# The long convolution of an H3 block recast from a 64x32 to a 128x16 split, with half of its shift filter moved to the tensor engine

## The chip, the cores and the metric

One core of one Trainium2 chip runs the whole program. The metric is device microseconds of one execution; lower is better. The old kernel took 296.26 us (median of 2 runs, 295.95 to 296.57). Engines are named as in the profile: PE is TensorE (matrix products), PEld its weight loads, DVE is VectorE, ACT is ScalarE, POOL is GpSimd, SP is the engine that issues most DMAs. "L498" is line 498 of the kernel that was run.

## The reference, cut to what matters

Four layers with residuals: mixer A, MLP B, A, B. The tensors are 2048 tokens by 512 channels, bf16. The convolution part of A depends on k, v and fixed weights, not on x, so both kernels compute it once and use it for both A layers.

```python
def _A_ref(q, k, v, shift_k, ssm_k, ssm_D):
    k_shift = sum over t in 0..3 of k_pad[:, t:t+S, :] * shift_k[:, 3-t]   # 4-tap causal filter
    kv = k_shift * v
    y = irfft(rfft(pad(kv)) * rfft(pad(ssm_k)))[:S]      # causal convolution of length 2048, per channel
    y = y + kv * ssm_D
    return q * y
def _B_ref(x, w1, b1, w2, b2):
    return gelu(layernorm(x) @ w1 + b1) @ w2 + b2        # 512 -> 1376 -> 512
x = x + A(layernorm(x)); x = x + B(layernorm(x)); x = x + A(...); x = x + B(...)
```

## The kernel before

The kernel records operations with declared durations, and a list scheduler written in the kernel file fixes the order of each engine before the program is built. So an edit can also re-order work. `A(p0, n, off, dims)` is a region of one big SBUF array, `P.op(engines, fn, duration, ...)` records one operation.

The convolution is a Fourier transform in two steps, as matrix products. A token index is 32c + a (c in 0..63, a in 0..31). Data sit as two groups of 64 partitions, so k and v are loaded in halves of 64 partitions:

```python
for g in range(2):
    dma(A(64 * g, 64, R_K + 1536, [1, 8192]), dr(A_k, 16 * g * 512, [32 * 512, 64], [1, 8192]), 1 << 20)
for g in range(2):
    dma(A(64 * g, 64, R_V, [1, 8192]), dr(A_v, 16 * g * 512, [32 * 512, 64], [1, 8192]), 1 << 20)
for j in range(8):
    tload(t_s2, 64 * 384, j * 3072, R_S2 + j * 3072, 3072)      # stage-two table, 6.3 MB
```

The shift filter runs on VectorE: seven tensor_tensor of 2048 columns and two of 1024 for each of four chunks:

```python
def shift_chunk(w):
    ...
    for j in range(3):
        tap(3 - j, tm[j])                       # multiply by one tap, 128x2048
    tt(tm[1], tm[0], tm[1], ALU.add, 1140.0)
    tap(0, tm[0])
    tt(tm[2], tm[1], tm[2], ALU.add, 1140.0)
    tt(tm[1], tm[2], tm[0], ALU.add, 1140.0)
    for h in range(2):
        tt(..., R_TMP ..., R_V ..., ALU.mult, 610.0)            # times v
    stage1(R_KP, R_GX + 8192 * (w // 2), 64, ..., EV_X)         # EV_X = (ACT,): evictions on ScalarE
```

Real and imaginary parts lie in columns of the same partition. Stage two takes three matmuls for each frequency, and the complex product takes two multiplies and an add and a subtract on VectorE:

```python
for i, t, gg in ins:                            # stage2, for each frequency
    e.matmul(Q(tl, 0, 128, i * 2 * n, [1, 2 * n]), t[0], gg[0], start=True, stop=False)
    e.matmul(Q(tl, 0, 128, i * 2 * n, [1, n]), t[1], gg[1], start=False, stop=False)
    r = e.matmul(Q(tl, 0, 128, i * 2 * n + n, [1, n]), t[2], gg[2], start=False, stop=True)
...
tt(po, x3, H, ALU.mult, 600.0)                  # products, for each 8 frequencies
tt(x3, x3, H_swapped_by_access_pattern, ALU.mult, 600.0)
for ri, p in ((0, po), (1, xo)):
    tt(R_Y ..., p[:32], p[32:], ALU.add if ri else ALU.subtract, 330.0)
```

After the inverse transform come the layer norms and the four MLP blocks per layer; the change leaves their arithmetic alone.

Of the kernel before, what the change touches and what calls it, by code (L numbers as in the profile page):

```python
# [7 lines left out]
ALU = mybir.AluOpType  # L8
# [371 lines left out]
def _tables():  # L380

    c = np.arange(64)[:, None]
    k1 = np.arange(64)[None, :]
    th = TWO_PI * c * (k1 + 0.5) / 128
    F = np.stack([np.cos(th), -np.sin(th)], -1).reshape(64, 128)
    F = np.concatenate([F, F], 0)
    a = np.arange(32)
    k2 = np.arange(32)
    f = np.arange(64)[:, None] + 0.5 + 128 * k2[None, :]
    th = TWO_PI * a[:, None, None] * f[None] / 4096  # L390
    tr = np.stack([np.cos(th), np.sin(th), -np.sin(th)], 2)
    S2 = np.zeros((32, 4, 64, 3, 32, 4))
    for d in range(4):
        S2[:, d, :, :, :, d] = tr
    S2 = S2.reshape(128, 64 * 3 * 128)
    ph = TWO_PI * k2[:, None] * a[None, :] / 32
    U = np.zeros((32, 4, 2, 32, 2, 4))
    for d in range(4):
        U[:, d, 0, :, 0, d] = np.cos(ph)
        U[:, d, 0, :, 1, d] = np.sin(ph)  # L400
        U[:, d, 1, :, 0, d] = -np.sin(ph)
        U[:, d, 1, :, 1, d] = np.cos(ph)
    U = U.reshape(128, 512)
    t = 32 * np.arange(64)[None, :] + a[:, None]
    ps = TWO_PI * t[None] * (np.arange(64)[:, None, None] + 0.5) / 4096
    T2 = np.stack([np.cos(ps), -np.sin(ps)], 2) / 2048
    T2 = T2.reshape(64, 4096)
    T2 = np.concatenate([T2, T2], 0)
    return F, S2, U, T2


AR = 105984


def bass_interleave_layers__ssm_conv_h3__mixer_channel_mlp__prompt_kernel(
# [3 lines left out]
    NS = 192  # L419
# [23 lines left out]
    def place(n):  # L443
        o = pos[0]
        pos[0] += n
        return o

    R_ID, R_F, R_D, R_B1, R_SJ3 = place(128), place(128), place(16), place(16), place(512)
    R_S2 = place(64 * 384)
    R_1, R_2, R_3, R_4, R_5, R_6 = (place(n) for n in (16384, 16384, 17920, 16384, 8192, 5120))  # L450
    assert pos[0] <= AR, pos[0]
    R_HRAW, R_HP, R_H = R_1, R_1 + 8192, R_1
    R_W1, R_W2 = R_1, R_1 + 5504
    R_GH, R_Z = R_2, R_2
    R_K, R_V, R_Y, R_U = R_3, R_3 + 19 * 512, R_3, R_3 + 16384
    R_GX, R_SR, R_X, R_T2 = R_4, R_4 + 12288, R_4, R_4 + 8192
    R_SJ = [R_4 + 8192 + 512 * w for w in range(3)] + [R_SJ3]
    R_KP, R_YT = R_5, R_5
    R_TMP, R_RING = R_6, R_6
    R_XT = R_S2  # L460
    R_HT = R_S2 + 4096
    R_N = R_S2 + 4096 + 2 * 5632
    M_B1, M_ST, M_MV, M_RS, M_HF = 0, 16, 16 + 96, 16 + 96 + 32, 16 + 96 + 32 + 16

# [4 lines left out]
    def dma(dst, src, nbytes, reads=(), prio=0.0, writes=None):  # L469
        return P.op(SP, lambda e: e.dma_start(dst, src, allow_slow_non_contiguous=True), 550.0, reads=reads,  # L470
                    writes=[dst] if writes is None else writes, dma=True, nbytes=nbytes, prio=prio)
# [7 lines left out]


    row = 128 + 128 + 512 + 4096
    P.op(ACT, lambda e: e.preload_act_table(AF.Gelu_apprx_tanh), 1300.0, prio=1e6)
    z = A(0, 1, R_K, [1, 1536])
    P.op(POOL, lambda e, z=z: e.memset(z, 0.0), 1300.0, writes=[z])
    tload(t_sm, row, 0, R_ID, 256)
# [3 lines left out]
    dma(A(0, 128, R_SR, [1, 2048]), dr(A_shift_k, 0, [0, 128], [1, 2048]), 1 << 19)  # L489
    dma(A(64, 64, R_K, [1, 1536]), dr(A_k, 13 * 512, [32 * 512, 64], [1, 1536]), 3 << 16)  # L490
    dma(A(1, 63, R_K, [1, 1536]), dr(A_k, 29 * 512, [32 * 512, 63], [1, 1536]), 3 << 16)
    for g in range(2):
        dma(A(64 * g, 64, R_K + 1536, [1, 8192]), dr(A_k, 16 * g * 512, [32 * 512, 64], [1, 8192]), 1 << 20)
    for g in range(2):
        dma(A(64 * g, 64, R_V, [1, 8192]), dr(A_v, 16 * g * 512, [32 * 512, 64], [1, 8192]), 1 << 20)
    for j in range(8):
        tload(t_s2, 64 * 384, j * 3072, R_S2 + j * 3072, 3072)

    HP = 0.0
    EV_H = EV_X = (ACT,)  # L500
    IDN = A(0, 128, R_ID, [1, 128])
    dconv, dx = Pool(2, 4), Pool(2, 2)
# [4 lines left out]
    P.op(POOL, lambda e: e.tensor_tensor(d0, d0, dd, ALU.add), 600.0, reads=[d0, dd], writes=[d0])  # L507
    for a4 in range(4):
        tl = Tile(dconv)
        for al in range(4):  # L510
            ins = []
            for b in range(4):
                for g in range(2):
                    src = A(0, 128, R_HRAW + b * 2048 + 16 * g + 4 * a4 + al, [32, 64])
                    ins.append((g, al * 512 + b * 128, src))

            def f(e, ins=ins, tl=tl):
                for g, o, src in ins:
                    r = e.transpose(QB(tl, 64 * g, 64, o, [1, 128]), src, IDN)
                return r  # L520
            P.op(PE, f, 8 * 60.0, reads=[x[2] for x in ins] + [IDN], tile=tl)
        dst = A(0, 128, R_HP + 16 * a4, [4, 4], [64, 128], [1, 4])

        def f(e, dst=dst, tl=tl):
            src = QB(tl, 0, 128, 0, [512, 4], [4, 128], [1, 4])
            if e is nc.scalar:
                return e.activation(dst, src, AF.Copy)
            return e.tensor_copy(dst, src)
        P.op((ACT, DVE), f, {ACT: 2048 * .833 + 60, DVE: 2048 * .52 + 70}, writes=[dst], tile=tl)

    def stage1(src, G, gk, gh, dg0, n, engs, prio=0.0):


        for d8 in range(dg0 // 8, (dg0 + n) // 8):
            for h in range(2):
                tl = Tile(dconv)
                ins = [(64 * g, i, A(64 * g, 64, src + (64 * h + 8 * d8 + i) * 64, [1, 64]), A(64 * g, 64, R_F, [1, 128]))
                       for i in range(8) for g in range(2)]

                def f(e, ins=ins, tl=tl):  # L540
                    for p, i, w, m in ins:
                        r = e.matmul(Q(tl, p, 64, i * 128, [1, 128]), w, m, start=True, stop=True)  # L542
                    return r
                P.op(PE, f, 16 * 45.0, reads=[x for y in ins for x in y[2:]], tile=tl, prio=prio)
                dst = A(0, 128, G + gh(h, 8 * d8), [gk, 128], [1, 8])

                def f(e, dst=dst, tl=tl):
                    src = Q(tl, 0, 128, 0, [1, 128], [128, 8])
                    if e is nc.scalar:
                        return e.activation(dst, src, AF.Copy)  # L550
                    return e.tensor_copy(dst, src)
                P.op(engs, f, {ACT: 1100.0, DVE: 1024 * 1.04 + 90}, writes=[dst], tile=tl, prio=prio)

    def stage2(G, ks, n, pool, prio=0.0):

        tl = Tile(pool)
        ins = []
        for i, k1 in enumerate(ks):
            g = G + k1 * 2 * n
            t = [A(0, 128, R_S2 + k1 * 384 + j * 128, [1, 128]) for j in range(3)]  # L560
            gg = [A(0, 128, g, [1, 2 * n]), A(0, 128, g + n, [1, n]), A(0, 128, g, [1, n])]
            ins.append((i, t, gg))

        def f(e):
            for i, t, gg in ins:
                e.matmul(Q(tl, 0, 128, i * 2 * n, [1, 2 * n]), t[0], gg[0], start=True, stop=False)  # L566
                e.matmul(Q(tl, 0, 128, i * 2 * n, [1, n]), t[1], gg[1], start=False, stop=False)  # L567
                r = e.matmul(Q(tl, 0, 128, i * 2 * n + n, [1, n]), t[2], gg[2], start=False, stop=True)  # L568
            return r
        P.op(PE, f, len(ks) * (4 * n * .42 + 10), reads=[x for _, t, gg in ins for x in t + gg[:1]], tile=tl, prio=prio)  # L570
        return tl

    stage1(R_HP, R_GH, 128, lambda h, dg: 64 * (dg // 32) + 32 * h + dg % 32, 0, 64, EV_H, HP)
    for k4 in range(16):
        tl = stage2(R_GH, range(4 * k4, 4 * k4 + 4), 128, dconv, HP)
        dst = A(0, 128, R_H + k4 * 1024, [1, 1024])

        def f(e, dst=dst, tl=tl):
            src = Q(tl, 0, 128, 0, [1, 1024])
            if e is nc.scalar:  # L580
                return e.activation(dst, src, AF.Copy)  # L581
            return e.tensor_copy(dst, src)  # L582
        P.op((ACT, DVE), f, {ACT: 1024 * .833 + 60, DVE: 1024 * 1.04 + 70}, writes=[dst], tile=tl, prio=HP)


    def tt(o, a, b, op, dur, eng=DVE):
        return P.op(eng, lambda e: e.tensor_tensor(o, a, b, op), dur, reads=[a, b], writes=[o])  # L587

# [4 lines left out]

    def shift_chunk(w):

        tm = [A(0, 128, R_KP + w * 1024, [64, 16], [4096, 2], [1, 64])]
        tm += [A(0, 128, o, [128, 16], [64, 2], [1, 64]) for o in (R_TMP, R_TMP + 2048)]

        def tap(j, o):
# [260 lines left out]
```

## Time and profile before

| stretch | what it is | what is full |
|---|---|---|
| 0 to 25.4 us | loads, filter transform begins | DMA |
| 25.4 to 121.5 us | convolution | VectorE, with ScalarE behind it |
| 121.5 to 295 us | layer norms and MLP | TensorE from 151 on |

The page of the old kernel, first its busy totals, then busy tenths in 40 slices of 7.4 us, and what the DMA engines moved in each slice:

```profile
PE 240.2 (81%) x2177; PEld 138.1 (47%) x2192; DVE 189.4 (64%) x401; ACT 143.0 (48%) x176; POOL 24.1 (8%) x43
DVE  0135999999999998898890794874938611101131
ACT  1069079598968469616327045152366321464000
GB/s 203 297 213 213 224 414 284 2 18 6 2 224 296 197 97 2 1 5 69 51 20 2 71 0 28 46 0 63 8 2 71 18 53 2 71 0 2 71 71 71
```

VectorE is at 8 or 9 tenths from the fifth to the sixteenth slice. In the table of stretches, the columns are busy time and instruction count of each engine, granted TensorE clock, DMA share and GB/s (two short rows between the stages are left out):

```profile
core 0: us, PE busy (x) PEld busy (x) DVE busy (x) ACT busy (x) POOL busy (x), PEclk, DMA share, GB/s
0.00:25.40 25.40, 11.83 (x256) 10.91 (x256) 3.82 (x7) 9.54 (x9) 1.88 (x7) 1.00 0.92 233
25.40:66.00 40.60, 25.70 (x474) 21.78 (x475) 39.88 (x39) 28.13 (x31) 0.96 (x2) 0.83 0.62 194
66.00:101.10 35.10, 30.02 (x554) 27.87 (x551) 34.73 (x65) 28.49 (x31) 1.04 (x2) 0.99 0.50 134
151.00:289.00 138.00, 137.26 (x612) 57.13 (x625) 64.58 (x163) 51.57 (x77) 10.81 (x18) 1.00 0.15 31
```

In the first row the DMA engines are busy for 0.92 of the time. VectorE then works 39.88 of 40.6 us and 34.73 of 35.1 us; from 151 to 289 TensorE works 137.26 of 138. What VectorE does, from the groups by form (count, then busy us and mean ns, then idle before them and its releaser):

```profile
L587 DVE TENSOR_TENSOR ar<-ar 128x512 bf16<-128x512 bf16 x96 | 35.1, 416 | 1.4 <-ACT ar L712 1.4
L587 DVE TENSOR_TENSOR ar<-ar 128x2048 bf16<-128x2048 bf16 x28 | 32.9, 1220 | 7.3 <-DMA ar<-in_A_k_dram 7.0
L587 DVE TENSOR_TENSOR ar<-ar 128x1024 bf16<-128x1024 bf16 x40 | 25.9, 683 | 0.2
L550 ACT ACTIVATE ar<-ps 128x1024 bf16<-128x1024 f32 x32 | 30.0, 1050 | 12.7 <-PE ps L542 12.7
```

Of the 96 adds and multiplies of 512 columns, 32 belong to the complex product. The 28 of 2048 columns are the shift filter. And from the timeline of VectorE and of ScalarE (start, length, group, idle before it and what ended that), where the shift filter begins and where the convolution's last evictions are:

```profile
25.38 38.18 DVE L587 TENSOR_TENSOR ar<-ar 128x2048 bf16<-128x2048 bf16 x36 [7.04 <-DMA ar<-in_A_k_dram]
...
114.10 7.44 ACT L712 ACTIVATE ar<-ps 128x1024 bf16<-128x1024 f32 x8 [0.74 <-PE ps L704]
```

The filter begins at 25.38 us, after waiting for k. The last eviction ends at 114.10 + 7.44 = 121.54 us.

### The profile page before, as it was taken

What the parts mean: (1) busy time and instruction counts of PE and PEld (TensorE: products, weight loads), DVE (VectorE), ACT (ScalarE), POOL (GpSimd) and SP (SyncE); (2) the same over time, 40 slices, a digit from 0 to 9 for tenths busy, and PEclk for the clock granted to TensorE, in tenths of its full rate; (3) what the DMA queues carried; (4) which work ended last, traced back from release to release, by engine and by line L of the source; (5) the groups of instructions that cost most, each with busy time, mean ns of one, the idle gap of its engine ahead of it and who ended that gap; (6) DMA issues with size and microseconds to landing.
All of it is one profiled execution on the core that took longest, in us unless ns stands there. A gap on an engine that the chain in (4) does not pass through costs nothing.

```text
span 295.0 us, 5161 instructions
## 1 busy us (share of the span) xinstructions
PE 240.2 (81%) x2177; PEld 138.1 (47%) x2192; DVE 189.4 (64%) x401; ACT 143.0 (48%) x176; POOL 24.1 (8%) x43
## 2 busy tenths in 40 slices
PE   0657086799899396329999999999999999999992
PEld 0655075588799284113433434434433444434440
DVE  0135999999999998898890794874938611101131
ACT  1069079598968469616327045152366321464000
POOL 2000000100010022210210110111101100000000
PEclk9999658999999879758999999999999999999997
DMA  6999997000099520003210301303003020200322
GB/s 203 297 213 213 224 414 284 2 18 6 2 224 296 197 97 2 1 5 69 51 20 2 71 0 28 46 0 63 8 2 71 18 53 2 71 0 2 71 71 71
DMA packets 22703, 25.75 MB, mean 87 GB/s; under 512 B 17722, under 2 KB 19355, under 8 KB 22170
## 3 DMA queue, kind: packets, MB, share of 16 engines
q1 hardware_dynamic: 22682, 25.44, 33.0%
q8 instruction: 17, 0.28, 0.4%
q14 instruction: 4, 0.03, 0.0%
HBM read 19.66 MB, written 2.10 MB: 74 GB/s over the span
## 4 chain that ended last, share of the span: by engine, by line
PE 51%; DVE 24%; DMA 10%; ACT 7%; SPq 2%; issue 2%; POOL 2%
PE ps L818 24%; PE ps L800 23%; DVE ar L587 16%; DMA ar<-in_A_v_dram 10%; DVE sm L729 3%; ACT ar L581 2%; SPq L470 2%; ACT ar L658 2%; DVE ar L743 2%; PE ps L650 2%; ACT ar L550 2%; ACT ar L627 1%; POOL sm L737 1%; DVE ar L582 1%; PE ps L566 1%
## 5 line engine op out<-in xcount | busy, mean ns | idle before, releaser
L805 ACT ACTIVATE ar<-ps,sm 128x512 bf16<-128x512 f32 (+1 forms) x88 | 59.5, 686 | 82.3 <-PE ps L800 59.1
L587 DVE TENSOR_TENSOR ar<-ar 128x512 bf16<-128x512 bf16 (+2 forms) x164 | 91.5, 618 | 8.9 <-DMA ar<-in_A_k_dram 7.0
L800 PE MATMUL ps<-ar 128*128 128x512 bf16 (+1 forms) x342 | 81.7, 385 | 1.6 <-ACT ar L789 1.2
L818 PE MATMUL ps<-ar 128*128 128x512 bf16 (+1 forms) x347 | 78.1, 379 | 0.8 <-DVE ar L822 0.6
L822 DVE TENSOR_TENSOR ar<-ar,ps 128x512 bf16<-128x512 bf16 x32 | 21.2, 682 | 65.5 <-PE ps L818 65.5
L800 PEld LDWEIGHTS ps<-ar 128*128 128x128 bf16 (+1 forms) x352 | 30.8, 101 | 50.8 <-ACT ar L805 21.4
L818 PEld LDWEIGHTS ps<-ar 128*128 128x128 bf16 (+1 forms) x352 | 33.6, 98 | 43.4 <-ACT ar L805 2.9
L729 DVE BATCH_NORM_STATS2 sm<-ar 128x6 f32<-128x512 bf16 x64 | 41.4, 681 | 0.1
L550 ACT ACTIVATE ar<-ps 128x1024 bf16<-128x1024 f32 x32 | 30.0, 1050 | 12.7 <-PE ps L542 12.7
L542 PE MATMUL ps<-ar 64*64 64x128 bf16 x512 | 21.6, 241 | 17.3 <-DVE ar L587 10.9
L566 PE MATMUL ps<-ar 128*128 128x128 bf16 (+1 forms) x192 | 30.0, 239 | 2.3 <-ACT ar L550 1.5
L743 DVE TENSOR_SCALAR ar<-ar,sm 128x512 bf16<-128x512 bf16 x64 | 23.2, 406 | 11.4 <-POOL sm L737 10.3
L568 PE MATMUL ps<-ar 128*128 128x64 bf16 (+1 forms) x192 | 29.2, 202 | 0.0
L567 PE MATMUL ps<-ar 128*128 128x64 bf16 (+1 forms) x192 | 29.1, 201 | 0.0
L542 PEld LDWEIGHTS ps<-ar 64*64 64x64 bf16 x512 | 17.9, 121 | 20.9 <-issue 9.1
L650 PE MATMUL ps<-ar 128*128 128x256 bf16 x128 | 17.7, 301 | 5.5 <-DVE ar L587 5.2
L566 PEld LDWEIGHTS ps<-ar 128*128 128x128 bf16 x192 | 18.7, 98 | 4.3 <-ACT ar L550 2.1
L568 PEld LDWEIGHTS ps<-ar 128*128 128x128 bf16 x192 | 18.8, 98 | 0.7
L650 PEld LDWEIGHTS ps<-ar 128*128 128x128 bf16 x128 | 15.7, 175 | 7.0 <-DVE ar L587 5.5
L567 PEld LDWEIGHTS ps<-ar 128*128 128x128 bf16 x192 | 18.8, 98 | 0.0
L627 ACT ACTIVATE ar<-ps 128x1024 bf16<-128x1024 f32 x16 | 15.9, 1043 | 3.3 <-DVE ar L587 3.1
L658 ACT ACTIVATE ar<-ps 128x1024 bf16<-128x1024 f32 x14 | 13.7, 1042 | 7.9 <-PE ps L650 7.9
(27 smaller groups left out, 97.0 us busy)
## 6 DMA issues: line engine op xcount, KB each, us to landing
ar<-tab_s SPq DMA_DIRECT2D x8, 768.0 KB, 34.1
ar<-in_A_ssm_k_dram SPq DMA_DIRECT2D x4, 512.0 KB, 5.5
ar<-in_A_k_dram SPq DMA_DIRECT2D x2, 1024.0 KB, 16.3
ar<-in_A_v_dram SPq DMA_DIRECT2D x2, 1024.0 KB, 25.9
ar<-in_A_q_dram SPq DMA_DIRECT2D x2, 1024.0 KB, 10.5
out_dram<-ar SPq DMA_DIRECT2D x8, 256.0 KB, 3.1
ar<-in_B_w_dram SPq DMA_DIRECT2D x1, 1376.0 KB, 8.5
ar<-in_B_w_dram SPq DMA_DIRECT2D x1, 1280.0 KB, 6.1
```

Of the source, the lines that this page charges most:

```text
L542: r = e.matmul(Q(tl, p, 64, i * 128, [1, 128]), w, m, start=True, stop=True)
L550: return e.activation(dst, src, AF.Copy)
L566: e.matmul(Q(tl, 0, 128, i * 2 * n, [1, 2 * n]), t[0], gg[0], start=True, stop=False)
L567: e.matmul(Q(tl, 0, 128, i * 2 * n, [1, n]), t[1], gg[1], start=False, stop=False)
L568: r = e.matmul(Q(tl, 0, 128, i * 2 * n + n, [1, n]), t[2], gg[2], start=False, stop=True)
L587: return P.op(eng, lambda e: e.tensor_tensor(o, a, b, op), dur, reads=[a, b], writes=[o])
L650: r = e.matmul(Q(tl, 0, 128, i * 256, [1, 256]), w, m, start=ri == 0, stop=ri == 1)
L729: P.op(DVE, lambda e, st=st, x=x: e.bn_stats(st, x), 600.0, reads=[x], writes=[st])
L743: P.op(DVE, lambda e: e.tensor_scalar(o, x, m, r, ALU.subtract, ALU.mult), 260.0, reads=[x, m, r], writes=[o])
L800: r = e.matmul(Q(tl, 0, rows, 0, [1, 512]), w, m, start=dk == 0, stop=dk == 3)
L805: P.op(ACT, lambda e, dst=dst, tl=tl, rows=rows, bias=bias: e.activation(dst, Q(tl, 0, rows, 0, [1, 512]), AF.Gelu_apprx_tanh, bias=bias), ...
L818: r = e.matmul(Q(tl, 0, 128, 0, [1, 512]), ins[fc][0], ins[fc][1], start=fc == 0, stop=fc == 10)
```

## The change

The token index becomes 16b + a (b in 0..127), so that every partition holds one block of 16 consecutive tokens and all loads span 128 partitions. Real parts lie on partitions 0-63, imaginary ones on 64-127, so stage two is one full 128x128 matmul for each frequency, with a table of 4 MB in place of 6.3. The complex product becomes two multiplies, by the spectrum H and by HS, a copy of it with the halves exchanged; the add and subtract are folded into the inverse matmul. HS is made by four 1 MB copies inside SBUF. Half of the channels (two of four blocks of 128) have their shift filter done on TensorE, with k transposed by the DMA and diagonal weight matrices. Evictions (the copies of finished sums out of PSUM, TensorE's output memory) of the first stage and of the products, on ScalarE alone before, may now go to VectorE too.

```diff
-R_K + 1536, two loads of 64 partitions;  R_V, two loads of 64 partitions
+    for i, c in enumerate(PE_CH):                     # PE_CH = (0, 1)
+        dst = A(0, 128, R_KT + i * 2064 + 16, [2048, 1], [1, 2048])
+        src = dr(A_k, 128 * c, [512, 2048], [1, 128])
+        P.op(SP, lambda e, dst=dst, src=src: e.dma_start_transpose(dst, src), 700.0, ...)
+    dma(A(0, 128, R_V, [1, 8192]), dr(A_v, 0, [16 * 512, 128], [1, 8192]), 1 << 21)
     ...
-                e.matmul(Q(tl, 0, 128, i * 2 * n, [1, 2 * n]), t[0], gg[0], start=True, stop=False)
-                e.matmul(Q(tl, 0, 128, i * 2 * n, [1, n]), t[1], gg[1], start=False, stop=False)
-                r = e.matmul(Q(tl, 0, 128, i * 2 * n + n, [1, n]), t[2], gg[2], start=False, stop=True)
+                r = e.matmul(Q(tl, 0, 128, i * n, [1, n]), w, m, start=True, stop=True)
     ...
+    for h in range(2):
+        for g in range(2):
+            src, dst = A(64 * g, 64, R_H + 8192 * h, [1, 8192]), A(64 - 64 * g, 64, R_HS + 8192 * h, [1, 8192])
+            dma(dst, src, 1 << 20, reads=[src])
+    def shift_pe(i):
+        ...
+                for a, j, w, m in ins:                # 8 tokens x 4 taps, 128x128 each
+                    r = e.matmul(Q(tl, 0, 128, a * 128, [1, 128]), w, m, start=j == 0, stop=j == 3)
+            ...
+                return e.tensor_tensor(o, Q(tl, ...), v, ALU.mult)     # VectorE, from PSUM
     ...
-            tt(A(0, 128, po, ...), x3, ..., ALU.mult, 600.0)
-            tt(x3, x3, ..., ALU.mult, 600.0)
-            for ri, p in ((0, po), (1, xo)):
-                tt(..., ALU.add if ri else ALU.subtract, 330.0)
+            for r in (R_H, R_HS):
+                h = A(0, 128, r + 8192 * hf + 64 * k16, [4, 16], [512, 16], [1, 4])
+                tt(h, x, h, ALU.mult, 660.0)
```

(Cut to the core; the tables, the memory layout and the last inverse stage change with it.)

## The prediction

> **What bounds the kernel now.** By the table of stretches there are three parts. (1) Loads, 0 to 25 us. (2) The convolution, 25 to 115 us: VectorE is busy 39.9 of 40.6 us in 25.4-66 and 35.6 of 36 in 66-102, ScalarE about 28 in each; the chain of waits names VectorE tensor_tensor through most of it. (3) Layer norms and MLP, 115 to 295 us: from 150 to 289 TensorE is busy 137.8 of 139 us. Part 3 is the same work after the change, so I take its 180 us as fixed.
>
> **What changes.** From the groups of instructions:
> - Shift filter on VectorE: 28 tensor_tensor of 2048 columns at 1.22 us = 34 us, plus 8 of 1024 at 0.68. Half goes to TensorE (128 matmuls, about 8 us by the 55-60 ns spacing of 128-column matmuls in the timeline). VectorE then multiplies from PSUM, 4 x about 1.2 us (its 1024-column PSUM copy takes 1.22). Saved: about 15 us of VectorE.
> - Complex products: 32 multiplies stay (22 us); 32 adds/subtracts of 0.416 us vanish, 13 us saved. TensorE does the sum.
> - PSUM evictions: 88 of 1024 columns before and after, 1.03 us on ScalarE, 1.22 on VectorE; more are allowed on VectorE.
> - TensorE in the convolution: one matmul per frequency, not three. Not limiting.
> - Added: four 1 MB copies inside SBUF that swap real and imaginary halves. Each spans 64 partitions. The trace moves 64-partition loads at 213 GB/s and 128-partition ones at 414; the Trainium skill, "SBUF - State Buffer", section "Door 1: The DMA port swizzle", says 64 partitions reach 8 of 16 ports, and the trace agrees. Estimate 5 us each, 20 us in all.
> - v (2 MB) now spans 128 partitions: 5 us, not 10. Stage table 4 MB, not 6.3: 5 us less. Half of k comes in by two DRAM transposes, estimate 4.2 us each (a burst of four 128 KB SBUF transposes took 4.8-5.1 us).
>
> **Critical path.** VectorE + ScalarE work in the convolution falls from about 170 to 142 us. I laid the trace's durations along each engine's static order. Shift on VectorE starts near 18 us, not 25. The last stage table lands near 41, not 48. The spectrum of the filter is ready at about 47; the first two swaps land near 59, and VectorE idles about 3 us there. The last two land near 69, idle again 1-2 us. Products end about 84 (before about 101), last eviction near 104 (before 121). The same sum for the old kernel gives 299 against 295 measured; new minus old is -19 us. Of 28 us of vector work, some is lost to waits for swaps and to inverse-stage evictions, now shared more evenly. I lean slightly cautious: -17.
>
> **Prediction: 279 us, 80% range 270 to 289. Faster by over 2%: 0.92; within 2%: 0.06; slower: 0.02.**
>
> **What would show each step.** tensor_tensor of 2048 columns: 28 -> 14; of 512: 96 -> 64. Shift's first VectorE multiply at 17-19 us. v lands near 31, transposes by 26. Swap copies issued near 47, landing 5 us apart. Products start near 59, with a wait of 2-5 us on the DMA. First layer-norm-stage evictions (inverse, last stage) end near 104. MLP still 140 us of saturated TensorE.
>
> **What would make it wrong.** DRAM transposes at 8 us each (+8 us). Swaps slower than 150 GB/s (+4), or the filter spectrum late because evictions queue behind shift work on in-order VectorE: everything in products waits for swaps. Strided weight loads on TensorE doubling a stage (+3 each). Multiplies with 4-element runs slower than 0.68 us (+0.3 us each x 32). Layer norm or weights arriving late would lengthen the supposedly fixed 180 us.

## The result, and the profile after

The new kernel took 273.78 us (median of 2 runs, 273.39 to 274.17), 22.5 us less than 296.26. A ratio here is the mean time of one kernel's runs over that of the other's runs of the same rounds, so it is not quite the ratio of the medians quoted: 0.9231, 95% interval 0.9173 to 0.9288. It lies in the predicted range, faster than the middle of it by 5 us.

The same views as before. The page:

```profile
PE 233.3 (86%) x2080; PEld 131.2 (48%) x2096; DVE 175.8 (65%) x362; ACT 131.7 (48%) x167; POOL 30.6 (11%) x57
DVE  0599999678999989989437848749659211101132
ACT  1396099657899842470551542533567030664000
GB/s 171 332 224 386 412 271 123 232 198 275 381 153 2 2 0 1 77 1 77 2 29 48 0 41 39 0 58 23 0 68 9 60 19 77 0 0 31 49 77 77
```

The stretches, cut where the stages of the new kernel lie (79.3 to 128.8 us left out):

```profile
0.00:15.50 15.50, 8.74 (x154) 8.24 (x156) 5.84 (x5) 5.31 (x6) 6.22 (x20) 1.00 0.90 252
15.50:52.20 36.70, 30.08 (x638) 26.32 (x632) 36.22 (x34) 27.34 (x31) 3.08 (x4) 1.00 0.93 277
52.20:65.00 12.80, 7.63 (x157) 6.85 (x158) 7.63 (x12) 6.82 (x8) 0.00 (x0) 0.74 0.97 206
65.00:79.30 14.30, 12.22 (x250) 11.75 (x248) 14.30 (x25) 13.12 (x15) 1.04 (x2) 0.88 0.92 330
128.80:266.70 137.90, 137.09 (x612) 57.17 (x625) 64.47 (x162) 51.67 (x77) 10.80 (x18) 1.00 0.14 31
```

VectorE is still full in the convolution (36.22 of 36.7 us, 14.30 of 14.3), except from 52.2 to 65, where it works 7.63 of 12.8 us. The MLP is the same saturated TensorE: 137.09 of 137.9 us. The groups:

```profile
L498 DVE TENSOR_TENSOR ar<-ar 128x512 bf16<-128x512 bf16 x64 | 23.2, 418 | 0.0
L498 DVE TENSOR_TENSOR ar<-ar 128x1024 bf16<-128x1024 bf16 x36 | 22.4, 699 | 3.7 <-issue 2.9 <-ACT ar L503 0.8
L498 DVE TENSOR_TENSOR ar<-ar 128x2048 bf16<-128x2048 bf16 x14 | 16.8, 1230 | 0.1
L504 DVE CAST ar<-ps 128x1024 bf16<-128x1024 f32 x16 | 19.0, 1231 | 1.4 <-PE ps L580 1.4
L627 DVE TENSOR_TENSOR ar<-ps,ar 128x1024 bf16<-128x1024 f32 x4 | 4.8, 1237 | 0.4 <-DMA ar<-in_A_v_dram 0.4
```

The counts are those predicted: 96 to 64, 40 to 36, 28 to 14, with four multiplies from PSUM at 1237 ns new. 16 evictions of 1024 columns now run on VectorE (7 before).

The timeline of VectorE, then of ScalarE and of the DMA queue of SP:

```profile
15.55 4.72 DVE L498 TENSOR_TENSOR ar<-ar 128x2048 bf16<-128x2048 bf16 x4
...
27.58 1.23 DVE L627 TENSOR_TENSOR ar<-ps,ar 128x1024 bf16<-128x1024 f32 x1 [0.38 <-DMA ar<-in_A_v_dram]
...
55.16 4.91 DVE L498 TENSOR_TENSOR ar<-ar 128x1024 bf16<-128x1024 bf16 x8 [2.94 <-issue]
...
64.75 14.54 DVE L498 TENSOR_TENSOR ar<-ar 128x1024 bf16<-128x1024 bf16 x24 [0.80 <-ACT ar L503]
```

```profile
90.63 7.44 ACT L503 ACTIVATE ar<-ps 128x1024 bf16<-128x1024 f32 x8 [1.13 <-PE ps L728]
```

```profile
42.94 7.80 SPq L487 DMA_DIRECT2D ar<-ar  x4
```

The shift filter begins at 15.55 us (25.38 before). VectorE's first multiply by v is at 27.58. The swaps are issued at 42.94; the first product waits 2.94 us and starts at 55.16. (The page puts that wait down to "issue"; the instruction's own waits are the two swap copies and its input's eviction; in e_add below the page puts the same wait down to the DMA, and the run without swaps removes it.) The last eviction ends at 90.63 + 7.44 = 98.07 us (121.54 before): 23.5 us earlier. From there to the end it is 173.5 us in both kernels (295.0 - 121.5, 271.6 - 98.1). So the whole gain is made in the loads and the convolution, and none is given back.

Two things changed together there: vector work went away, and work began earlier. The experiments separate them.

### The profile page after: what moved, and what is told of

Read it like the earlier page. It is cut to its first block, busy times and chain, and to the rows that moved or that the text cites. A ratio compares the mean times of both kernels' runs of the same rounds, so it can differ in the third digit from the quotient of the medians.

```text
span 271.6 us, 4924 instructions
## 1 busy us (share of the span) xinstructions
PE 233.3 (86%) x2080; PEld 131.2 (48%) x2096; DVE 175.8 (65%) x362; ACT 131.7 (48%) x167; POOL 30.6 (11%) x57
## 4 chain that ended last, share of the span: by engine, by line
PE 57%; DVE 24%; DMA 7%; ACT 5%; issue 3%; POOL 2%; SPq 1%; DVEq 0%; ACTq 0%
PE ps L835 26%; PE ps L817 25%; DVE ar L498 11%; DVE sm L746 6%; DMA ar<-ar 5%; ACT ar L503 5%; PE ps L620 3%; DVE ar L504 3%; DVE ar L760 2%; POOL sm L754 2%; PE ps L565 2%; DMA ar<-in_A_ssm_k_dram 2%; PE ps L580 1%; DVE sm L748 1%; DVE ar L839 1%
## 5 line engine op out<-in xcount | busy, mean ns | idle before, releaser
L503 ACT ACTIVATE ar<-ps 128x1024 bf16<-128x1024 f32 x72 | 67.5, 1045 | 27.4 <-PE ps L593 11.1
L498 DVE TENSOR_TENSOR ar<-ar 128x512 bf16<-128x512 bf16 (+2 forms) x114 | 62.4, 606 | 3.8 <-issue 2.9
L760 DVE TENSOR_SCALAR ar<-ar,sm 128x512 bf16<-128x512 bf16 x64 | 23.3, 406 | 11.4 <-POOL sm L754 10.3
L580 PE MATMUL ps<-ar 128*64 128x128 bf16 x512 | 20.1, 231 | 8.8 <-ACT ar L503 7.0
L593 PE MATMUL ps<-ar 128*128 128x64 bf16 (+1 forms) x384 | 19.2, 215 | 4.2 <-issue 1.7
L580 PEld LDWEIGHTS ps<-ar 128*64 128x64 bf16 x512 | 16.4, 116 | 12.2 <-ACT ar L503 9.5
L593 PEld LDWEIGHTS ps<-ar 128*128 128x128 bf16 x384 | 17.6, 107 | 5.8 <-DVE ar L504 2.3
L504 DVE CAST ar<-ps 128x1024 bf16<-128x1024 f32 x16 | 19.0, 1231 | 1.4 <-PE ps L580 1.4
L754 POOL TENSOR_TENSOR sm<-sm 128x4 f32<-128x4 f32 x16 | 16.9, 1059 | 1.3
L681 PE MATMUL ps<-ar 128*128 128x128 bf16 x256 | 15.0, 220 | 0.1
L681 PEld LDWEIGHTS ps<-ar 128*128 128x128 bf16 x256 | 14.5, 114 | 0.3 <-ACT ar L503 0.2
L565 PE MATMUL ps<-ar 128*128 128x128 bf16 x64 | 5.9, 270 | 6.5 <-POOL ar L550 6.5
L504 DVE COPY ar<-ps 128x2048 bf16<-128x2048 bf16 x4 | 4.8, 1229 | 9.7 <-PE ps L565 9.7
L798 PE MATMUL ps<-ar 128*128 128x128 bf16 x16 | 2.1, 309 | 9.6 <-DVE ar L760 9.6
```

The source lines that it names most:

```text
L498: return P.op(eng, lambda e: e.tensor_tensor(o, a, b, op), dur, reads=[a, b] + list(more), writes=[o])
L503: return e.activation(dst, src(), AF.Copy)
L504: return e.tensor_copy(dst, src())
L580: r = e.matmul(Q(tl, 64 * ri, 64, i * 128, [1, 128]), w, m, start=True, stop=True)
L593: r = e.matmul(Q(tl, 0, 128, i * n, [1, n]), w, m, start=True, stop=True)
L681: r = e.matmul(Q(tl, 0, 128, i * 128, [1, 128]), w, m, start=q == 0, stop=q == 1)
```

## The experiments

The theory: the convolution is a chain from the loads through a full VectorE, so both the vector work taken off and the earlier loads count nearly one for one; the swaps cost a few us back. Rivals: only the vector work counts (A); only the earlier loads count (B); the gain is the freedom to evict on either engine (C).

Every job also timed the old kernel on the same chip: medians 297.38, 296.98, 296.84 and 297.05 us. I compare ratios to it, and turn a difference of ratios into us by 297. The new kernel's own ratio is 0.9231, from only two runs, so each such difference carries about 1.7 us either way from that interval alone, and about 2 with the variant's own; differences below that are no result. All variants run four times.

| run | what it does | median us | ratio | against the new kernel, us |
|---|---|---|---|---|
| a_pe0 | no block on TensorE | 280.16 | 0.9411 | +5.3 |
| a_pe1 | one block | 279.77 | 0.9439 | +6.2 |
| a_pe3 | three blocks | 285.68 | 0.9603 | +11.0 |
| e_add | adds and subtracts put back | 283.63 | 0.9545 | +9.3 |
| e_noswap | swaps left out | 269.22 | 0.9069 | -4.8 |
| e_delay | loads of k, v, table about 10 us later | 284.49 | 0.9578 | +10.3 |
| e_vhalf | v in two half-partition loads | 280.10 | 0.9439 | +6.2 |
| b_both | old kernel, first-stage evictions on both | 298.83 | 1.0066 | (old kernel +2.0) |
| e_swap8 | swaps in eight pieces | 274.85 | 0.9253 | +0.7 |
| e_swap2q | half of the swaps on ScalarE's queue | 274.37 | 0.9251 | +0.6 |
| e_swpool | half of the swaps on GpSimd's queue | 276.37 | 0.9312 | +2.4 |
| e_swap128 | same bytes, 128 partitions, no swap | 269.86 | 0.9076 | -4.6 |

The comparison with the reference does not notice an error in this small branch. Apart from the chip, in double precision, the new chain of tables gives the causal convolution to a relative error of 3e-14 with the swap, and is off by 0.86 without it.

### e_add: the removed adds and subtracts

"Pinned" here and below means that the declared durations were left alone, and the order of each engine was compared and found the same but for the edit.

```diff
-                tt(h, x, h, ALU.mult, 660.0)          # for r == R_HS
+                def f(e, h=h, x=x, u=u, v=v, t=t):
+                    e.tensor_tensor(t[0], u, v, ALU.add)          # 128x512, into unused columns
+                    e.tensor_tensor(t[1], u, v, ALU.subtract)
+                    return e.tensor_tensor(h, x, h, ALU.mult)
+                P.op(DVE, f, 660.0, reads=[x, h], writes=[h])
```

> Order of every engine pinned; 32 dummy add/subtract of 512 columns (0.34 us each, 10.7 us in all) put back into the product stage, output unchanged. Theory A: 279 to 285 us (the product stage is VectorE-bound; at most some 4 us of idle before it can hide part). If the removed add/subtract were not on the critical path: 273 to 275.

```profile
58.23 0.69 DVE L498 TENSOR_TENSOR ar<-ar 128x1024 bf16<-128x1024 bf16 x1 [4.64 <-DMA ar<-ar]
58.85 0.42 DVE L674 TENSOR_TENSOR ar<-ar 128x512 bf16<-128x512 bf16 x1
59.18 0.42 DVE L675 TENSOR_TENSOR ar<-ar 128x512 bf16<-128x512 bf16 x1
59.52 0.68 DVE L676 TENSOR_TENSOR ar<-ar 128x1024 bf16<-128x1024 bf16 x1
```

Measured: +9.3 us for 10.7 us of vector work (each add or subtract puts off the next instruction by 0.33 to 0.34 us, 32 times). The product stage is VectorE-bound, and rival B falls.

### a_pe0, a_pe1, a_pe3: how much of the shift filter on TensorE

```diff
-PE_CH = (0, 1)
+PE_CH = ()          # a_pe0;  (0,) is a_pe1;  (0, 1, 2) is a_pe3
```

> The changed kernel with the whole shift filter on VectorE (no channels on TensorE); the scheduler re-plans. Theory A (the gain is vector work taken off a VectorE-bound convolution): VectorE gets back 14 tensor_tensor of 2048 columns (16.8 us) and 4 of 1024 (2.8), and loses 4 PSUM multiplies (4.8), net +14.8 us; part of it is absorbed by moving evictions to ScalarE, so 280 to 287 us against 273.8. Theory B (the gain is earlier loads): the two DRAM transposes of k vanish and v lands some us earlier, so 270 to 274.

> One channel block of four on TensorE instead of two, re-planned. Between none (280.2) and two (273.8) if vector work alone counts: 276 to 278. If the second DRAM transpose in front of v costs about as much as its block of vector work saves: 271 to 275.

> Three of four channel blocks on TensorE instead of two; re-planned. Theory A read naively: 7 us less vector work, so 267 to 272. My expectation from the old order: a third DRAM transpose (about 3.5 us) delays v and the stage table, TensorE takes 4 us more of shift work in front of the filter spectrum, and VectorE starves early, so slower: 277 to 290.

Measured: +5.3 for none, +6.2 for one, +11.0 us for three. The half that the change moves is worth about 5 us of the 22.5, a third of the 14.8 us of vector work that it takes off. The first block moved gives nothing that can be seen, the second gives it all, and a third takes twice that away. My expectation for one block (271 to 278 by one theory or the other) missed. These runs are re-planned by the scheduler, so they show what the choice is worth in this program, not the price of one block. Nor is it vector work alone. The filter's first multiply in a_pe0, then in a_pe1:

```profile
19.14 4.63 DVE L498 TENSOR_TENSOR ar<-ar 128x2048 bf16<-128x2048 bf16 x4 [1.26 <-DMA ar<-in_A_k_dram]
```

```profile
18.95 4.63 DVE L498 TENSOR_TENSOR ar<-ar 128x2048 bf16<-128x2048 bf16 x4 [2.26 <-DMA ar<-in_A_k_dram]
```

Both start over 3 us later than the new kernel's 15.55, because VectorE waits for more of k. How much of the 5 us is this later start was not tested.

In the timeline of VectorE in a_pe3, two waits can be read off:

```profile
59.23 1.30 DVE L498 TENSOR_TENSOR ar<-ar 128x1024 bf16<-128x1024 bf16 x2 [9.27 <-DMA ar<-ar]
...
72.80 0.69 DVE L746 BATCH_NORM_STATS2 sm<-ar 128x6 f32<-128x512 bf16 x1 [5.31 <-DMA ar<-in_A_q_dram]
```

With little shift work left, VectorE sits 9.27 us until the swaps land, and then 5.31 us for q, because the plan put layer-norm statistics of q ahead of the remaining products on an engine that runs in order. The extra matmuls did not delay the swaps, which are issued at 42.73 us (42.94 in the new kernel); but the re-planned order loads MLP weights ahead of them (the weights' 2752-byte packets move from 40 to 48 us in the DMA records). The lack of work to cover the swaps, and the new order, are what the trace shows. I did not test the two apart.

### e_delay and e_vhalf: the loads

```diff
+        for i, t in enumerate((A_q, A_v)):            # e_delay: 4 MB ahead of k, to a region not yet used
+            x, y = A(0, 128, R_4 + 8192 * i, [1, 8192]), dr(t, 0, [16 * 512, 128], [1, 8192])
+            P.op(SP, lambda e, x=x, y=y: e.dma_start(x, y), 0.0, writes=[x], dma=True, nbytes=0)
```

> Order pinned; two idle 2 MB loads put in the queue ahead of k, so k, v and the stage table come about 10 us later, near the old kernel's times (shift's first multiply at 25 us instead of 15.6). Theory: after k lands VectorE and ScalarE are busy almost without a gap, so the 10 us go nearly whole into the time: 281 to 285 us against 273.8. Rival (load times do not matter, only vector work): 273 to 276.

```profile
26.84 4.63 DVE L498 TENSOR_TENSOR ar<-ar 128x2048 bf16<-128x2048 bf16 x4 [11.89 <-DMA ar<-in_A_k_dram]
```

Measured: the shift filter starts at 26.84 instead of 15.55 us, 1.5 us later than in the old kernel, and the time rises by 10.3 us. So the load time counts nearly in full (10.3 us for a start 11.3 us later), and rival A falls too. With its loads about as late as the old kernel's, the new kernel takes 284.49 us. Scaled to the 9.8 us by which the new kernel really starts earlier, the loads are worth about 9 of the 22.5 us (an estimate).

```diff
-    dma(A(0, 128, R_V, [1, 8192]), dr(A_v, 0, [16 * 512, 128], [1, 8192]), 1 << 21)
+    for g in range(2):                                # e_vhalf
+        x, y = A(64 * g, 64, R_V, [1, 8192]), dr(A_v, 64 * g * 16 * 512, [16 * 512, 64], [1, 8192])
+        P.op(SP, lambda e, x=x, y=y: e.dma_start(x, y), 0.0 if g else 550.0, writes=[x], dma=True,
+             nbytes=0 if g else 1 << 21)
```

> Order pinned; v loaded as two 64-partition transfers as in the old kernel. If each runs at 213 GB/s as there, v and the stage table land 5 us later; VectorE waits for v at 27.6 with almost no slack and the filter spectrum waits for the table, so +3 to +5 us: 277 to 279. If the 64-partition form is not slower here: 273 to 275.

```profile
33.41 1.22 DVE L630 TENSOR_TENSOR ar<-ps,ar 128x1024 bf16<-128x1024 f32 x1 [4.61 <-DMA ar<-in_A_v_dram]
```

Measured: +6.2 us. VectorE's first multiply by v starts at 33.41 instead of 27.58 us after a wait of 4.61. (In this profiled run the filter itself began 1.7 us later than in the new kernel's, before any edited transfer, so about 4 us of the delay are v's.) This one layout choice, the same bytes over 64 or 128 partitions, is worth about a quarter of the gain. The Trainium skill, "SBUF - State Buffer", section "Door 1: The DMA port swizzle", says that 64 partitions reach only 8 of the 16 ports; the run agrees: v's packets of 16 KB took 1.30 us each against 0.61 in the new kernel (medians in the DMA records).

### b_both: evictions on either engine

```diff
-    EV_H = EV_X = (ACT,)
+    EV_H = EV_X = (ACT, DVE)          # in the old kernel
```

> The old kernel with its first-stage evictions allowed on both engines (they were ScalarE only), re-planned. Rival C (the new kernel gains because evictions may go to either engine): 280 to 288 us. My theory (VectorE is full there, so it can take none): 293 to 299, no verdict of faster.

Measured: 0.7% slower (ratio 1.0066, interval 1.0034 to 1.0099). Rival C falls for the old kernel: its VectorE has no room for evictions. It moved only three more of them there in sum. The product evictions stayed on ScalarE, and no run took the freedom away from the new kernel, so what it is worth there is not shown.

### e_noswap, e_swap8, e_swap2q, e_swpool, e_swap128: the swaps

```diff
-            dma(dst, src, 1 << 20, reads=[src])
+            # e_noswap: 64 of 8192 columns, same declared regions and size
+            P.op(SP, lambda e, ds=ds, ss=ss: e.dma_start(ds, ss), 550.0, reads=[src], writes=[dst], dma=True, nbytes=1 << 20)
```

> Wrong result on purpose: the four 1 MB half swaps copy only 64 columns each, order pinned. If the swaps cost what the trace suggests (VectorE idle 2.9 us before the first product): 268 to 272 us. If they are hidden: 273 to 275. If they cost more than their visible wait, through delayed weight and q loads: below 268.

```profile
52.52 4.91 DVE L498 TENSOR_TENSOR ar<-ar 128x1024 bf16<-128x1024 bf16 x8
```

Measured: -4.8 us. The first product starts at 52.52 us with no wait, where the new kernel waits until 55.16. So the change pays about 5 us for the swaps, more than the visible 2.94 us wait: the next few us of evictions and products bunch behind it (7.63 of 12.8 us busy, in the table of stretches). From 43 to 64 us, first the new kernel, then e_noswap, VectorE is busy 16.51 and 20.24 us:

```profile
43.00:64.00 21.00, 12.89 (x314) 10.86 (x309) 16.51 (x19) 14.29 (x16) 0.00 (x0) 0.87 0.96 203
```

```profile
43.00:64.00 21.00, 15.04 (x404) 12.18 (x400) 20.24 (x27) 18.86 (x21) 0.00 (x0) 1.00 0.71 238
```

Three attempts to get it back:

```diff
-    for h in range(2):
+    for kh in range(2):               # e_swap8: eight copies of 0.5 MB, by frequency half
+      for h in range(2):
...
-            dma(dst, src, 1 << 20, reads=[src])
+            dma(dst, src, 1 << 20, reads=[src], eng=ACT if g else SP)      # e_swap2q; POOL in e_swpool
```

> A version meant to beat both: the swaps cut in eight of 0.5 MB by frequency half, so that the first four can start when half of the filter spectrum is evicted; re-planned. If the 4.8 us that the swaps were seen to cost are mostly the wait for whole 1 MB copies: 269 to 272 us. If the port rate of the copies sets it, or the 512-byte runs are slower: 273 to 277.

> Two of the four swaps (those from partitions 64-127) are issued from ScalarE's DMA queue, so that copies in both directions are in flight at once; nearly the same order (two evictions change engines). If one copy is limited by the half of the ports it reaches, two opposite copies together move about twice 213 GB/s and all four land some 10 us after the issue: 269 to 272 us. If they share the same engines and serialize, as the Trainium skill (SBUF - State Buffer, section on issuing two DMAs) says of two loads: 274 to 280, with ScalarE held up at the issue.

> The same, but the two swaps are issued from GpSimd's queue, so ScalarE is not held up; GpSimd waits for the first to land before it issues the second. If opposite copies overlap: 269 to 272 us. If they serialize: 273 to 278.

All three missed: +0.7, +0.6 and +2.4 us. In e_swpool GpSimd issued its second copy only at 59.34 us, after it had waited 15.26 us for its first. In e_swap8 the first products do start sooner, but the later ones wait:

```profile
64.73 14.54 DVE L498 TENSOR_TENSOR ar<-ar 128x1024 bf16<-128x1024 bf16 x24 [5.67 <-DMA ar<-ar]
```

5.67 us of idle: the first half came early, a weight load slipped into the queue between, and 4 MB at about 190 GB/s (512-byte packets in the trace's DMA records) end no sooner: the last packet at 69.3 us, against 65.0 in the new kernel. In e_swap2q copies in both directions were in flight at once, and moved no more. The stretch of 43 to 53 us, first the new kernel, then e_swap2q, last e_swap128 (last column GB/s):

```profile
43.00:53.00 10.00, 6.98 (x198) 5.68 (x194) 9.15 (x9) 9.19 (x10) 0.00 (x0) 1.00 0.94 198
```

```profile
43.00:53.00 10.00, 7.21 (x168) 6.10 (x169) 9.05 (x9) 7.00 (x9) 0.00 (x0) 0.83 0.95 205
```

```profile
43.00:53.00 10.00, 7.86 (x215) 6.34 (x212) 9.93 (x11) 9.29 (x11) 0.22 (x2) 1.00 0.78 243
```

205 GB/s against 198. The Trainium skill, "SBUF - State Buffer", section "Can I just issue two DMAs to hit both halves?", says that two transfers to the two halves serialize, measured there at only +6%; this agrees (+4%), although here they came from two queues and each read one half while it wrote the other.

```diff
+            if g == 0:                # e_swap128: 2 MB over 128 partitions, partition to partition; wrong result
+                ds, ss = A(0, 128, R_HS + 8192 * h, [1, 8192]), A(0, 128, R_H + 8192 * h, [1, 8192])
+            else:                     # a token copy
+                ds, ss = A(0, 64, R_DG + 64 * h, [1, 64]), A(64, 64, R_H + 8192 * h, [1, 64])
```

> Wrong result on purpose (no swap of halves), order pinned: the same 4 MB go from the filter spectrum to the swapped buffer as two 2 MB copies over all 128 partitions, partition to partition, in place of four 1 MB copies from one half to the other. If the 64-partition shape is what holds the swaps to about 210 GB/s, the packets move at 350 to 420 GB/s and the time is 269 to 272 us, near the run without swaps. If any copy inside SBUF is held to about 210 GB/s: 273 to 276 us, and about 20 us of copying remain.

Measured: -4.6 us, as good as no swaps at all. The packets of 16 KB took 0.84 us each (median in the DMA records) against 1.28 in the new kernel; with 16 engines, 16 x 16 KB / 0.84 us is 312 GB/s against 205. (From the first packet to the last, gaps and other loads included, the 4 MB took 14.5 us, which is 289 GB/s.) So it is not the bytes but the half-to-half shape that makes the swaps late. The run changed two things at once, the span of 64 partitions and the crossing from one half to the other, and does not tell them apart; nor did the full shape reach the 350 to 420 GB/s that I had expected of it. Such a copy cannot exchange halves, so this is a measurement and not a better kernel. No run beat the new kernel with a right result.

## Why the prediction was right, and where it was off

| point | predicted | measured |
|---|---|---|
| time | 279 (270 to 289) | 273.78 |
| part 3 unchanged | same in both | 173.5 us in both from the last eviction |
| 2048-column multiplies and adds | 28 to 14 | 28 to 14 |
| 512-column | 96 to 64 | 96 to 64 |
| shift filter starts | near 18 us | 15.55 |
| v there (first multiply by it) | near 31 | 27.58 |
| swaps issued | near 47 | 42.94 |
| first product | near 59, after a 3 us wait | 55.16, after 2.94 |
| products end | near 84 | 79.29 (64.75 + 14.54) |
| last eviction | near 104 | 98.07 |

The mechanism was right in the main: VectorE was the limit, the MLP does not change, and the swaps cost a wait of the size foretold. Of the vector work taken off, e_add shows the adds and subtracts worth 9.3 of their 10.7 us; the shift filter's 14.8 us brought a third of their size. The prediction said that some would be lost to waits, but not which.

The term that was mis-sized is the load stage. The prediction said "v lands near 31, transposes by 26" and "swap copies issued near 47". The swaps went out 4 us before that, and what came after kept that lead or gained on it (5.9 us at the last eviction). Two parts of the estimate were too long. The transposes were put at 4.2 us each, but the 4096 packets of 256 bytes that they make took 5.4 us for both (from the DMA records: 14.35 to 19.79 us). And I had laid transfers of tiny runs strictly one after another, where the DMA records show 8-byte, 512-byte and 2048-byte packets in the same 3 us, from 9 to 12. One part was too short: v's own packets ran from 19.75 to 27.03 us, 7.3 us and not 5. On top of that I turned the summed -19 us into -17 "slightly cautious", in the wrong direction.

What the prediction did not weigh is how the gain divides. It spoke of "28 us of vector work" as the gain and of loads only as start times. The runs say: later loads +10.3, adds and subtracts +9.3, half of the shift filter on TensorE about +5 (its earlier start included), swaps -4.8. These sum to about 20 of the 22.5 us; each was measured alone against the new kernel, so they need not add up and overlap in the loads, and what the single matmul per frequency and the rest of the layout give was not measured by itself. The named feature of the change, the filter on TensorE, is the smaller part.

"Swaps slower than 150 GB/s" did not happen (about 205), "Strided weight loads on TensorE doubling a stage" did not (the 128 shift matmuls were busy 8.2 us, foretold 8), and "multiplies with 4-element runs slower than 0.68" hardly: 36 of 1024 columns (the 32 products and four of the shift filter) took 699 ns on average.

## What to carry to other kernels

When one engine is full from the moment its data arrive, a microsecond of load time costs about as much as a microsecond of its work (here 10.3 us for 11.3, and 9.3 for 10.7): look at how tensors lie over the partitions before moving arithmetic between engines. Measure the parts of a compound change one at a time with the order pinned; here the filter on TensorE was worth about a quarter of the gain. Price a copy between partition halves at the half-partition rate, and keep other work ready to cover it.

## What the Trainium skill lacked or had wrong

- "DMA: Bandwidth & Descriptors", section "Where 436 GB/s comes from", says that for transfers between HBM and SBUF the HBM side (about 358) binds, and for copies inside SBUF the fabric side (435). Here, with one core running, it is the other way about: loads over 128 partitions ran at 413 GB/s (stretch 27 to 33 us of the new kernel), and copies inside SBUF over 128 partitions at 312 GB/s by packet time (e_swap128). The same section calls a 425 GB/s measurement of its own near the fabric rate; the 413 agrees with that figure and not with a limit of 358.
- "SBUF - State Buffer", section "Door 1: The DMA port swizzle", gives rates of half-partition transfers by port count. It does not say what a copy from one half to the other does: 205 GB/s here by packet time, and 205 in the stretch with both directions in flight on two queues. Inside SBUF, 128 partitions straight against half to half was a factor of 1.5; for the loads of v, 128 against 64 partitions was 2.1, close to the 2 of the port count.
- "DMA: Bandwidth & Descriptors", section "Latency and other measured facts", gives 261 GB/s for a DMA transpose with a non-contiguous middle dimension. The transposes of k from HBM, with 256-byte rows, moved 189 GB/s in the stretch 15 to 18 us, which is mostly theirs. The section has no figure for a transpose of 256-byte source rows.
